# Row-tiled low query products, h read in PSUM, weights' words through ScalarE and a PSUM bank, and a new order list

## The chip, the cores and the metric

One program runs on one core of a Trainium2 chip. The metric is the device time of one execution in microseconds (us). The core's engines work side by side, each through its own queue in order: TensorE (PE), VectorE (DVE), ScalarE (ACT), GpSimd (POOL) and SyncE (SP, which here issues DMAs). SBUF is the big on-chip memory, PSUM the small one that TensorE writes, in banks of 512 f32 words per partition.

## The reference, cut to what matters

```
q_pool = q.reshape(B, H, S//2, 2, D).mean(axis=3)            # B=4, H=8, S=1152, D=64
scores = (q_pool @ k^T) / 8                                    # 576 x 1152 for each head
attn   = softmax(scores) ;  x = attn @ v                       # 2304 tokens x 512
h = x @ w_in                                                   # 512 -> 2048
P = a0 + a1 h + a2 h^2 + a3 h^3 ;  Q = 1 + |b0||h| + |b1| h^2
y = (P / (Q + 1e-6)) @ w_out                                   # 2048 -> 512
e = argmax(y @ w_gate) ;  gate = softmax(...)[e] ; eom = sigmoid(y @ w_output_gate)[e]
out = gate * eom * (relu(y @ w1[e]) @ w2[e])                   # top-1 of 8 experts, 512 -> 1024 -> 512
```

The arithmetic is that of f32: each f32 operand is cut into a high and a low f16 part, and a product is the sum of high·high, high·low and low·high.

## The kernel before, in words

**Attention** runs in 144 units. A unit is one head's 128 queries against all 1152 keys, and two neighbouring units (t = 0 and 1) are the two heads of a pair; 128 units are of this kind, and 16 ("m" units) hold the last 64 queries of two heads, each with its own 64 columns of TensorE. A unit's 1024 first scores go to one of two score buffers of two banks each (`sab`, in turn; line 718), the last 128 to a third bank (`shared`). VectorE finds their maximum (lines 728 and 731), ScalarE or VectorE makes the bias (738, 740), ScalarE takes exp (746). The exponentials are cut into high (`ph`, 755/757) and low (`pl`, 761), transposed by a DMA that SP issues (763), and multiplied by v (770). K and q are likewise cut (520 high, 526 low) and transposed by DMA (529). K's high and low lie one above the other in the 128 contraction rows, so a unit takes q_high against both, and q_low against both: four matmuls of 512 columns, each with all 128 rows.

**The first expert layer** takes 18 tiles of 128 tokens, each in 4 groups of 512 hidden columns, 72 groups in all. A group's h comes from 48 small matmuls (1148 to 1150) in one of two banks `hps`. It is copied to SBUF (1189, on ScalarE or VectorE). The numerator's steps `lin`, `tt` and `next_` (1172/1174, 1163, 1184 to 1187) work on that copy, on VectorE, GpSimd or (lin) ScalarE, while ScalarE takes Abs, Square, Ln and Exp in the PSUM bank itself (1197 to 1203). Three more VectorE steps (1159) follow, then the cut into gh and gl (1207, 1163) and the product with w_out (1215 to 1217). The weights are stored as 64-bit floats, and three VectorE steps over 1024 words turn a chunk into f32 (881, 884, 888; 16 chunks, 48 instructions); high and low parts follow.

**The second expert layer** works on 128 tokens of one expert at a time ("slots"). Some come while the first layer runs; 14 late slots follow at the end, in plain code: 96 matmuls of 128 columns (1476 to 1478), ReLU (1483) and its rest (1484) over 1024 columns, 24 matmuls of 512 columns (1494 to 1496), the gate (1506), and an indirect DMA of the rows (1500). Beside them the next expert's weights are sized (478, an all-reduce on GpSimd at 1443, the scale at 1422 to 1424) and cut (500, 511).

**What sets the order.** Up to the late slots every engine follows one long list, `ORDER`: each entry is an engine's letter (T for TensorE, V for VectorE, A for ScalarE, G for GpSimd, S for SP) and a number of a step, and the list both chooses the engine of a step and its place. Waits between engines come from what steps read and write. TensorE does not reorder: a matmul that waits holds up those behind it.

Of the kernel before, what the change touches and what calls it, by code (L numbers as in the profile page):

```python
# [9 lines left out]
F32 = mybir.dt.float32  # L10
F16 = mybir.dt.float16
BF16 = mybir.dt.bfloat16
I32 = mybir.dt.int32
AF = mybir.ActivationFunctionType
ALU = mybir.AluOpType
# [7 lines left out]
G2 V4 S7 A96 G97 V3 S0 V1 A11 V12 V13 V14 S38 V15 V16 S37 S8 V17 V18 S30 V39 V40 V86 V41 A42 V87 G88 A90 V19 V20 V21  # L23
V22 S52 V23 V24 A89 V43 S51 V25 V26 V53 S31 S9 A120 V27 V32 V28 V54 V33 V29 S10 S44 S65 S66 V55 V121 S45 V34 A123 V124
A56 V57 S91 A35 V4018 V36 S6 V67 V46 A93 V68 V47 V48 A49 V69 A70 S58 V94 V50 S59 S79 V71 S80 S126 A155 S95 T109 V60
V61 V81 V62 A63 V156 V82 S73 V64 V83 S72 V74 V75 V76 A84 S158 A184 V185 A77 S125 A152 S92 S213 V78 T98 V100 T99 V101
S5 A102 A103 A104 A105 T110 V111 S214 G153 V215 S122 T127 V112 V113 V216 A114 G394 T128 A115 S157 V129 G106 S220 V130
A181 V217 A131 A132 V85 T138 A116 G117 V140 A218 T139 V141 A133 S154 A142 A143 V4019 T159 T160 A144 V182 T170 A395
A397 S221 V222 V223 V287 V161 G396 A398 V219 V162 S107 A134 A163 S227 V224 S228 V229 V230 A225 S118 V135 V231 V226
A145 V146 A165 S234 S235 V236 A232 V237 S4017 g233 V4022 S183 T108 T119 A164 T171 V172 V173 V174 S241 T188 V190 A176  # L30
S242 S187 S136 A175 T189 S147 V191 A1079 V238 S255 S248 V192 g166 V243 V244 A239 T199 V201 T137 T148 S249 A177 V167
S168 A193 T200 V245 S263 V149 V202 V150 V151 A194 A246 V203 V240 V247 G178 V250 V251 V252 V274 S256 S399 S179 V273
A204 V275 V276 A205 A195 G196 T402 T401 V257 V258 S186 V1080 A253 T169 V254 S262 A206 g207 T180 S1082 V259 A1076 g1077
V403 V404 V405 A406 T412 V414 V278 T413 V277 A260 A407 V279 V280 T423 S197 T198 A408 V264 V265 S208 V409 V266 A267
# [12 lines left out]
V687 V688 V697 T352 A689 V681 T353 T696 G370 T545 S671 A690 V546 S682 V547 g691 T371 T372 G692 V548 A1072 V698 T709
A549 V699 A700 V550 T373 T374 T672 T710 A701 A702 G703 A375 G391 T720 V711 V712 V713 T376 A715 S551 V722 A377 V286
T683 T378 A714 T721 V716 V379 V723 S693 V724 S704 T731 A725 G717 A726 T552 V380 V381 V382 T383 V733 V727 T694 T553
A384 T732 V385 A386 T573 T742 V734 V735 A736 G728 V387 A737 T743 V389 G738 G739 V390 V744 T705 V706 T869 V745 A746  # L50
A747 A748 T554 T555 V707 V871 V708 S718 T719 A556 T870 A557 V1304 A559 T880 A558 V872 V873 T574 G749 g750 A874 A562
S1074 A1305 A875 A563 V392 V882 T881 V883 V884 V560 T575 S729 T576 V577 A578 T891 V388 G1306 A886 g393 g876 S740 G877
T730 S1107 T902 S751 V561 A885 T892 V564 V565 A580 T741 S878 V566 V893 V894 A567 S1310 A1307 T594 T595 A579 T596 T597
A887 A1308 V895 A896 T903 A897 V1137 G1138 A583 A598 A898 T752 V888 S889 T916 V904 V905 A906 V581 g899 V568 V753 A599
T569 A907 A584 g601 V754 V755 T879 V918 A908 V582 S1142 S900 S1139 A756 T917 g757 S758 V919 V585 A909 T927 V586 A920
g910 A921 A922 g923 T928 V587 A600 T890 V929 V930 T570 V931 A604 T938 A605 T615 V602 T571 V606 T616 T572 A588 A932
g589 S911 T939 A933 V603 A1108 T901 V940 A934 g935 V924 V607 V941 A942 A943 V608 T949 V951 A609 G1464 V1109 A944 S925
A1166 T590 T617 T950 T591 S1309 T592 G610 V952 V953 T618 V619 A945 A620 g622 T759 T912 A954 A955 A956 V1167 T1083 S936
# [285 lines left out]
def whole(tc, general, keep, checked, q, k, v, w_in, w_out, moe_a, moe_b, w_gate, w_ogate, w1, w2, out):  # L344
# [1309 lines left out]
    if not general:  # L1654
        make_fixed(-7)
# [213 lines left out]
```

## Time and profile before

| | us |
|---|---|
| runs | 1105.92, 1108.17, 1108.96 (median 1108.17) |
| profiled execution: time | 1104.09 |
| profiled execution: span of the trace | 1102.2 |
| TensorE busy | 923.3 (84%) |
| VectorE busy | 868.2 (79%) |
| ScalarE busy | 726.6 (66%) |
| GpSimd busy | 566.3 (51%) |

The mean granted clock of TensorE is 0.951. The shares are means over stages: a start of 55 us, attention with the first layer up to about 860 us, and the late slots. TensorE's matmuls overlap, and a matmul's printed duration (0.38 us for 512 columns) is longer than the distance from one start to the next (0.22 us).

### The profile page before, as it was taken

The page shows a single profiled execution, that of the slowest core. Times are in us where ns is not written, and L with a number is a line of the kernel's source. Part 1 is how long each engine was busy: PE and PEld are TensorE (multiplying, and loading weights), DVE is VectorE, ACT ScalarE, POOL GpSimd, SP SyncE. Part 2 cuts the span into 40 slices and gives each one's busy share as a digit, 9 for nine tenths or more (in the row PEclk, how much of TensorE's full clock was granted, in tenths as well). Part 3 has the DMA queues.
Part 4 walks back from the last instruction along what each step waited for, and adds up shares of the span by engine and source line. Part 5 has one row for each costly group of instructions (what it writes and reads, how often), then busy time and mean ns, then how long its engine had stood idle before and what let it go on. Part 6 is the DMA issues. An engine that isn't in the chain of part 4 may idle for free. (4 is left out here: it accounts for less than half of the span.)

```text
span 1102.2 us, 30178 instructions
## 1 busy us (share of the span) xinstructions
PE 923.3 (84%) x12138; PEld 660.7 (60%) x12138; DVE 868.2 (79%) x1727; ACT 726.6 (66%) x1132; POOL 566.3 (51%) x396
## 2 busy tenths in 40 slices
PE   0144678877789999999998889999999998999984
PEld 0022555655557766777776657677777675776742
DVE  6998888888888999998998998998898843333452
ACT  2364578777779888898887888899877511222222
POOL 1034267785568766667776567686845611010110
PEclk9955699999899999999999999999999999999997
DMA  8899999999999999899999999999864324333530
GB/s 300 269 252 286 222 194 190 195 212 210 203 191 172 208 186 203 170 158 179 158 193 178 188 171 187 218 152 163 145 111 147 76 59 98 78 73 74 174 87 17
DMA packets 493493, 185.91 MB, mean 169 GB/s; under 512 B 454596, under 2 KB 473028, under 8 KB 493253
## 3 DMA queue, kind: packets, MB, share of 16 engines
q1 hardware_dynamic: 490365, 174.26, 81.5%
q0 software_dynamic: 2960, 9.46, 2.5%
q8 instruction: 99, 1.62, 0.6%
q14 instruction: 69, 0.57, 0.2%
HBM read 60.45 MB, written 11.82 MB: 66 GB/s over the span
## 5 line engine op out<-in xcount | busy, mean ns | idle before, releaser
L1148 PE MATMUL hps<-scr,winh 128*128 128x128 f16 x1152 | 210.1, 222 | 9.1 <-DVE scr L1159 7.0
L1149 PE MATMUL hps<-scr,winh 128*128 128x128 f16 x1152 | 210.0, 222 | 0.0
L1150 PE MATMUL hps<-scr,winl 128*128 128x128 f16 x1152 | 209.9, 222 | 0.0
L761 POOL TENSOR_TENSOR att<-att 128x1152 f16<-128x1152 f32 x69 | 169.3, 2453 | 52.3 <-ACT att L755 27.6
L718 PE MATMUL sab<-att 128*128 128x512 f16 x512 | 138.9, 397 | 54.0 <-DMA att<-att 46.5
L728 DVE TENSOR_REDUCE small<-sab 128x1 f32<-128x1024 f32 x144 | 175.1, 1217 | 10.9 <-PE sab L718 8.1
L770 PE MATMUL shared<-att 128*128 128x65 f16 (+3 forms) x4320 | 151.0, 198 | 38.9 <-DMA att<-att 21.5
L770 PEld LDWEIGHTS <-att 128*128 128x128 f16 (+1 forms) x4320 | 141.0, 103 | 65.0 <-DMA att<-att 32.0
L746 ACT ACTIVATE att<-sab,small 128x1024 f32<-128x1024 f32 x144 | 159.9, 1111 | 12.8 <-DVE small L740 9.5
L718 PEld LDWEIGHTS <-att 128*128 128x128 f16 x768 | 69.8, 101 | 143.8 <-issue 62.2
L1149 PEld LDWEIGHTS <-winh 128*128 128x128 f16 x1152 | 113.8, 99 | 27.7 <-issue 11.6
L1163 POOL TENSOR_TENSOR scr<-scr 128x512 f16<-128x512 f32 (+1 forms) x77 | 103.4, 1345 | 48.3 <-ACT scr L1207 18.2
L1148 PEld LDWEIGHTS <-winh 128*128 128x128 f16 x1152 | 114.5, 99 | 19.5 <-issue 2.2
L1150 PEld LDWEIGHTS <-winl 128*128 128x128 f16 x1152 | 113.8, 99 | 0.0
L1476 PE MATMUL sab<-att 128*128 128x128 f16 x608 | 106.0, 221 | 7.0 <-DMA att<-att 4.9
L1215 PE MATMUL yps<-wouth,scr 128*128 128x512 f16 x288 | 109.9, 381 | 2.0 <-DVE small L493 1.4
L1217 PE MATMUL yps<-wouth,scr 128*128 128x512 f16 x288 | 109.8, 381 | 1.7 <-POOL scr L1163 1.3
L1216 PE MATMUL yps<-woutl,scr 128*128 128x512 f16 x288 | 109.8, 381 | 0.0
L1478 PE MATMUL sab<-att 128*128 128x128 f16 x608 | 105.9, 221 | 2.4 <-DVEq L1732 1.8
L1477 PE MATMUL sab<-att 128*128 128x128 f16 x608 | 105.9, 221 | 0.0
L1500 POOL DMA_INDIRECT out_dram<-att x19 | 19.0, 997 | 164.3 <-ACTq L1732 116.3
L755 ACT CAST att<-att 128x1152 f16<-128x1152 f32 x66 | 76.1, 1153 | 20.3 <-DMA att<-att 19.5
(219 smaller groups left out, 2250.9 us busy)
## 6 DMA issues: line engine op xcount, KB each, us to landing
att<-in_k_dram SPq DMA_DIRECT2D x16, 576.0 KB, 5.0
att<-in_q_dram SPq DMA_DIRECT2D x16, 512.0 KB, 4.7
att<-in_moe_w_dram SPq DMA_DIRECT2D x4, 2048.0 KB, 8.9
att<-in_v_dram SPq DMA_DIRECT2D x14, 576.0 KB, 4.8
scr<-in_moe_w_out_dram SPq DMA_DIRECT2D x12, 512.0 KB, 4.7
att<-ysort SPq DMA_DIRECT2D x19, 257.0 KB, 2.7
scr<-in_moe_w_in_dram SPq DMA_DIRECT2D x8, 512.0 KB, 8.5
woutl<-in_moe_w_in_dram SPq DMA_DIRECT2D x6, 512.0 KB, 7.5
```

The lines of the kernel that those rows point to most:

```text
L718: T.matmul(dst[:, d0:d0 + w], qT[:, H * x + 2 * i + t, :], rhs, start=(x == 0), stop=(x == 1))
L728: A(key - ahead - .6, {"DVE": 1.13}, lambda e: V.tensor_reduce(out=mm[:, 0, bi:bi + 1], in_=ab, axis=AX.X, op=MAX, negate=True), r=[f"sab{ ...
L746: return lambda e: S.activation(dst, src, AF.Exp, bias=mm[:, 2, bi:bi + 1], scale=escale)
L761: lambda e: eng(e).tensor_tensor(out=phs[pb][:, 1], in0=p32, in1=ph(), op=SUB),
L770: T.matmul(pvb[p0:p0 + w, bi, 0:d], pt[:, lhs, p0:p0 + w], rhs[:, h, c, :], start=(c == 0 and lhs == 0 and rhs is vh), stop=(lhs == 2 * KC ...
L1148: T.matmul(hp, wh, xh[:, kc, :], start=(kc == 0), stop=False)
L1149: T.matmul(hp, wh, xl[:, kc, :], start=False, stop=False)
L1150: T.matmul(hp, wl, xh[:, kc, :], start=False, stop=(kc == KD - 1))
L1215: T.matmul(yps, a, wouth[:, ff, :], start=(ff == 0), stop=False)
L1216: T.matmul(yps, a, woutl[:, ff, :], start=False, stop=False)
L1217: T.matmul(yps, b_, wouth[:, ff, :], start=False, stop=(ff == KF - 1))
L1476: T.matmul(o, a, xT[:, kc], start=(kc == 0), stop=False)
```

## The change

It is one diff with several parts:

- Weights' words: a chunk is worked in two halves of 512. ScalarE makes the exponent's offset from the top 16 bits, one VectorE step writes into the PSUM bank `yps`, a second reads it back and writes f32 to SBUF. So a chunk takes two ScalarE and four VectorE instructions of 512 words for three VectorE instructions of 1024.
- Groups: the copy of h is gone; `lin`, `tt` and `next_` read the PSUM bank, `tt` and `next_` on VectorE alone, `lin` on ScalarE or VectorE. Abs goes from the bank to SBUF, Square and Ln stay there, Exp comes back to the bank. A token `hx` keeps readers of the same bank one after the other.
- Scores: K's parts are laid out so that head 0 has its high part in rows 0 to 63 and head 1 in rows 64 to 127. `high` is q_high against all 128 rows, as before. `low` is q_low against K's high part alone, 64 rows: head 0 from rows 0 to 63 into `sab0`, head 1 from rows 64 to 127 into `sab1`, matmul by matmul in turn. The low products of both heads stand with the second head's high ones in one step. The product low·low is dropped. For the first 128 queries of a batch q_low is not doubled.
- Late slots: the first product comes in two halves in alternate banks, with ReLU and rest for each half of 512; the scale of the next weights is made with their cut (`[2 * p:...]`) and not with their size, so a slot's VectorE steps no longer stand behind the all-reduce; the last slot's rows are written by an indirect DMA at the very end of the program, in both branches of its last If.
- Constants are set in two steps, and the index tables lie in another buffer.
- `ORDER` is a new list.

```diff
-V22 S52 V23 V24 A89 V43 S51 V25 V26 V53 S31 S9 A120 V27 V32 V28 V54 V33 V29 S10 S44 S65 S66 V55 V121 S45 V34 A123 V124
+A3386 V3113 V2907 A3107 T2921 T2922 V3108 A2908 A2909 S3083 T3062 V2910 A2923 A2924 V3063 V3114 G3092 T2753 T2754
...
+            kn4 = nrm.rearrange("p (c x d) -> p c x d", c=KC, x=4)
...
+            A(key + .4, {"DVE": 0.73, "ACT": 1.15, "POOL": 1.25}, as16(kn4[:, :, 0:4:3, :], krc), r=tk, w=tn)
+            A(key + .5, {"DVE": 1.33, "POOL": 2.5}, rest(kn4[:, :, 1:3, :], krc, kn4[:, :, 0:4:3, :]), r=tk + tn, w=tl)
...
+        def high(dst, h, ps, stop=False):
...
+                    T.matmul(dst[:, d0:d0 + w], qT[:, 2 * i + h, :], krow(h, c0, w), start=True, stop=False)
...
+        def low(dsts, ps):
+            for c0, w in ps:
+                d0 = c0 % 1024
+                for h, dst in dsts:
...
+                        T.matmul(dst[:, d0:d0 + w], qT[64 * h:64 * h + 64, lo, :], krow(h, c0, w, 64 * h, 64),
+                                 start=False, stop=True)
...
-        A(key - ahead - 1.2, {"PE": 0.86 * f2}, smm(ab, [(0, 512), (512, 512)]), r=ins, w=[f"sab{par}"])
...
+        elif t == 0:
+            A(key - ahead - 1.2, {"PE": 0.43}, lambda e: high(sab[0], 0, main), r=ins, w=["sab0"])
+            A(key - ahead - 1.1, {"PE": 1.06},
+              lambda e: (high(sab[1], 1, main), low([(0, sab[0]), (1, sab[1])], main)), r=ins, w=["sab1", "sab0"])
...
+                return [lambda e: S.activation(hx.bitcast(U16)[:, 0:1024:2], top, AF.Copy, scale=2.0**-13, bias=2.0**-14 - 0.5),
+                        lambda e: V.scalar_tensor_tensor(out=ax, in0=high[:, cs], scalar=3, in1=hx,
+                                                         op0=ALU.logical_shift_left, op1=ALU.bitwise_xor),
+                        lambda e: V.scalar_tensor_tensor(out=di[:, cs], in0=high[:, cs], scalar=-0x80000000, in1=ax,
+                                                         op0=ALU.bitwise_and, op1=ALU.bitwise_xor)]
...
-        A(k2, {"ACT": 0.48, "DVE": 0.6}, lambda e: (S.copy if e == "ACT" else V.tensor_copy)(tq, hb),
-          r=[ht], w=[f"tq{tb}"], port=0)
...
-        A(k2 + .04, LP, lin, r=[f"tq{tb}", c], w=[f"tp{tb}"])
-        A(k2 + .045, {"POOL": 1.24, "DVE": 0.6}, tt(tp, tp, tq, MUL), r=[f"tq{tb}"], w=[f"tp{tb}"])
-        A(k2 + .05, {"POOL": 1.9, "DVE": 0.65}, next_, r=[f"tq{tb}", c], w=[f"tp{tb}"])
+            A(k2 + .01, {"ACT": 0.57}, lambda e: S.activation(te, hb, AF.Abs, scale=cf("sh")), r=[ht, c], w=[tk] + hx)
...
+            A(k2 + .03, {"ACT": 0.62, "DVE": 0.6}, lin, r=[ht, c], w=[pk] + hx, port=0)
+            A(k2 + .04, {"DVE": 0.6}, tt(tp, tp, hb, MUL), r=[ht], w=[pk] + hx)
+            A(k2 + .05, {"DVE": 0.65}, stt(tp, tp, lambda: cf("n1"), hb, ADD, MUL), r=[ht, c], w=[pk] + hx)
...
+            A(k2 + .07, {"ACT": 0.5}, lambda e: S.activation(hb, lg, AF.Exp, scale=-1.0), r=["lg"] + hx, w=[ht])
...
+            steps = mms_[0:4] + relu(halves[0], 0, 512) + mms_[4:8] + relu(halves[1], 512, 512)
...
-                do(wsplit(s, x)[3 * p:None if p else 3])
+                do(wsplit(s, x)[2 * p:None if p else 2])
...
+    with short.Else():
+        do([({"POOL": 1.05}, put_last)])
```

On VectorE, near the program's start, the first chunks of weights' words stand like this before (lines 881, 884 and 888 are the three steps, 526 a low part):

```order
L881 TENSOR_SCALAR scr<-woutl 128x1024
L884 SCALAR_TENSOR_TENSOR scr<-woutl,scr 128x1024
L632 TENSOR_TENSOR att<-att 128x8x64
L888 SCALAR_TENSOR_TENSOR scr<-woutl,scr 128x1024
L522 CAST att<-att 128x8x64
L493 RECIPROCAL small<-small 128x1
L493 TENSOR_SCALAR small<-small 128x1 x4
L493 TENSOR_REDUCE small<-small 128x1
L526 TENSOR_TENSOR winl<-scr,winh 128x1024
```

And now, at the same place of VectorE's order:

```order
L943 SCALAR_TENSOR_TENSOR yps<-wouth,att 128x512
L478 TENSOR_REDUCE small<-small 128x1
L945 SCALAR_TENSOR_TENSOR scr<-wouth,yps 128x512
L943 SCALAR_TENSOR_TENSOR yps<-woutl,att 128x512
L945 SCALAR_TENSOR_TENSOR scr<-woutl,yps 128x512
L943 SCALAR_TENSOR_TENSOR yps<-woutl,att 128x512
L945 SCALAR_TENSOR_TENSOR scr<-woutl,yps 128x512
L478 TENSOR_REDUCE small<-winh 128x1
L511 SCALAR_TENSOR_TENSOR winl<-scr,winh 128x1024
```

The second step of a half reads the bank that the first has just written, and the next half writes it again, so these steps follow one another in one chain. Before the first `TENSOR_REDUCE` of scores stand 33 such half steps, 7 low parts of w_in and 3 of K or v; before the change there were 24 whole steps, 7 low parts of w_in and 5 of K or v.

On TensorE, in the middle of the attention, the scores of a unit stand between second products of the first layer before (`sab0_74` and `sab1_75` are the two score buffers):

```order
L1217 MATMUL yps_79<-wouth_72,scr_83 128x512
L718 LDWEIGHTS att_81
L718 MATMUL sab0_74<-att_81 128x512
L718 LDWEIGHTS att_81
L718 MATMUL sab0_74<-att_81 128x512
L718 LDWEIGHTS att_81
L718 MATMUL sab0_74<-att_81 128x512
L718 LDWEIGHTS att_81
L718 MATMUL sab0_74<-att_81 128x512
L1215 LDWEIGHTS scr_83
```

And now the second step of a pair of units, whose two other high products into `sab0_74` stand further up:

```order
L741 LDWEIGHTS att_81
L741 MATMUL sab1_75<-att_81 128x512
L741 LDWEIGHTS att_81
L741 MATMUL sab1_75<-att_81 128x512
L752 LDWEIGHTS att_81
L752 MATMUL sab0_74<-att_81 128x512
L752 LDWEIGHTS att_81
L752 MATMUL sab1_75<-att_81 128x512
L752 LDWEIGHTS att_81
L752 MATMUL sab0_74<-att_81 128x512
L752 LDWEIGHTS att_81
L752 MATMUL sab1_75<-att_81 128x512
```

Four full matmuls for one unit have become six for the second half of a pair, the last four of them on 64 rows and into the two buffers in turn; `sab0` is complete only when this step is.

On VectorE, in a late slot, this stood before (478 sizes the next weights, 1422 to 1424 make their scale, 1484 is the rest of ReLU):

```order
L478 TENSOR_REDUCE small<-winh 128x1
L1422 TENSOR_SCALAR small<-small 128x1
L1423 TENSOR_SCALAR small<-small 128x1
L1424 TENSOR_SCALAR small<-small 128x1
L1732 UNCONDITIONAL_BRANCH x2
L1484 SCALAR_TENSOR_TENSOR att<-sab_75,att 128x1024
L1485 TENSOR_SCALAR small<-att,small 128x1
```

And now:

```order
L478 TENSOR_REDUCE small<-att 128x1
L1827 UNCONDITIONAL_BRANCH x2
L1563 SCALAR_TENSOR_TENSOR att<-sab_74,att 128x512
L1563 SCALAR_TENSOR_TENSOR att<-sab_75,att 128x512
L1572 TENSOR_SCALAR small<-att,small 128x1
L1826 TENSOR_LOAD att
L1826 ISA x2
L1827 COMPARE_AND_BRANCH
L1500 TENSOR_SCALAR small<-small 128x1
```

The scale's three steps have moved from ahead of the slot's rest to behind it, and the rest comes in two halves.

Over the part that the list orders, the steps that moved most are (instructions before and after): on VectorE `pl` 47 and 23, `ph` 15 and 9, low parts of K and v of 1152 columns 22 and 13, `tt` 44 and 72, `next_` 58 and 72, `lin` 18 and 28, copies of h 16 and 0, evacuations of `yps` (1322, 1328) 16 and 8; on ScalarE copies of h 56 and 0, `ph` 102 and 72, `lin` 30 and 44, words 0 and 32; on GpSimd `pl` 97 and 121, `ph` 27 and 63, parts of K and v of 1152 columns 10 and 25, and 80 steps of groups (`lin`, `tt` and the two of `next_`) to none.

## Rows read from the trace of the kernel before

**Rows 1.** Windows: stretch, length, busy PE, PEld, DVE, ACT, POOL, clock, DMA share, GB/s:

```profile
0.00:55.00 55.00, 3.79 (x10) 1.52 (x11) 45.00 (x74) 18.41 (x20) 4.28 (x11) 0.97 0.86 284
55.00:300.00 245.00, 170.28 (x2305) 118.56 (x2304) 207.66 (x368) 170.39 (x258) 138.72 (x81) 0.84 1.10 218
300.00:860.00 560.00, 533.26 (x7490) 387.25 (x7491) 515.43 (x1059) 478.05 (x781) 387.52 (x273) 0.99 0.96 174
860.00:1080.00 220.00, 207.77 (x2313) 150.56 (x2310) 95.92 (x223) 58.13 (x75) 34.82 (x32) 0.99 0.37 86
1080.00:1103.00 23.00, 8.17 (x24) 2.80 (x24) 4.20 (x7) 1.63 (x3) 0.97 (x1) 0.70 0.05 13
```

**Rows 2.** Groups of TensorE, 55 to 300: busy, mean ns, idle before, what ended it:

```profile
L770 PE MATMUL shared<-att 128*128 128x65 f16 (+3 forms) x1269 | 49.0, 204 | 30.2 <-DMA att<-att 18.2 <-DVE small L731 5.3 <-DMA att<-scr 4.6
...
L718 PE MATMUL shared<-att 128*128 128x128 f16 x78 | 11.6, 235 | 20.5 <-ACT att L746 18.2 <-DMA att<-scr 1.8 <-DVE small L493 0.4
```

**Rows 3.** Line 728: ns min/median/max, first and last start:

```profile
L728 DVE TENSOR_REDUCE small<-sab x144: 1193/1217/1225, 55.5 to 808.2; 128x1 f32<-128x1024 f32 x144
```

**Rows 4.** Time line of VectorE (start us, duration us, what), first weights' words:

```profile
14.59 0.69 DVE L881 TENSOR_SCALAR scr<-woutl 128x1024 int32<-128x1024 int32 x1
15.32 1.22 DVE L884 SCALAR_TENSOR_TENSOR scr<-woutl,scr 128x1024 int32<-128x1024 int32 x1
```

**Rows 5.** Time line of TensorE, first matmuls ([idle before <-what ended it]):

```profile
44.13 3.57 PE L718 MATMUL sab<-att 128*128 128x512 f16 x8 [44.13 <-DMA att<-att]
```

**Rows 6.** Time line of TensorE, one unit's scores:

```profile
424.16 1.03 PE L718 MATMUL sab<-att 128*128 128x512 f16 x4
```

**Rows 7.** Time line of TensorE, the scores of an m unit:

```profile
488.99 0.38 PE L1217 MATMUL yps<-wouth,scr 128*128 128x512 f16 x1
489.29 1.05 PE L715 MATMUL sab<-att 128*64 128x512 f16 x8
490.28 0.39 PE L1215 MATMUL yps<-wouth,scr 128*128 128x512 f16 x1
```

**Rows 8.** Groups of VectorE by shape, 0 to 860:

```profile
L1187 DVE SCALAR_TENSOR_TENSOR scr<-scr,small 128x512 f32<-128x512 f32 x56 | 55.2, 986 | 0.2
...
L1159 DVE SCALAR_TENSOR_TENSOR scr<-scr,hps 128x512 f32<-128x512 f32 x70 | 47.9, 684 | 1.6
L761 DVE TENSOR_TENSOR att<-att 128x1152 f16<-128x1152 f32 x31 | 46.7, 1506 | 1.9 <-ACT att L755 1.9
...
L1174 DVE TENSOR_SCALAR scr<-scr,small 128x512 f32<-128x512 f32 x18 | 12.7, 703 | 2.5 <-ACT scr L1189 1.3 <-POOL scr L761 1.1
...
L1322 DVE TENSOR_SCALAR yr<-yps 128x512 f32<-128x512 f32 x9 | 6.2, 686 | 2.0 <-PE yps L1217 1.9
```

**Rows 9.** Groups of ScalarE by shape, 0 to 860:

```profile
L746 ACT ACTIVATE att<-sab,small 128x1024 f32<-128x1024 f32 x144 | 159.9, 1111 | 12.8 <-DVE small L740 9.5 <-DVE small L493 1.2 <-DVE att L761 1.1
L755 ACT CAST att<-att 128x1152 f16<-128x1152 f32 x66 | 76.1, 1153 | 20.3 <-DMA att<-att 19.5 <-ACT att L746 0.2
...
L1189 ACT COPY scr<-hps 128x512 f32<-128x512 f32 x55 | 32.2, 586 | 22.0 <-PE hps L1150 21.7
```

**Rows 10.** Groups of GpSimd by shape, 0 to 860:

```profile
L761 POOL TENSOR_TENSOR att<-att 128x1152 f16<-128x1152 f32 x69 | 169.3, 2453 | 52.3 <-ACT att L755 27.6 <-DVE att L757 8.6 <-DVE scr L1163 2.5
...
L1163 POOL TENSOR_TENSOR scr<-scr 128x512 f32<-128x512 f32 x28 | 39.3, 1405 | 8.8 <-DVE scr L1174 4.4 <-DVE small L493 2.2 <-DVE hps L1159 1.5
```

**Rows 11.** Time line of TensorE, the late slots:

```profile
1053.75 0.22 PE L1476 MATMUL sab<-att 128*128 128x128 f16 x1 [3.18 <-DMA att<-att]
...
1081.82 0.39 PE L1494 MATMUL hps<-att 128*128 128x512 f16 x1 [2.25 <-ACTq L1732]
...
1083.86 0.61 PE L1496 MATMUL hps<-att 128*128 128x512 f16 x1 [1.31 <-DVE att L1484]
...
1090.92 0.38 PE L1496 MATMUL hps<-att 128*128 128x512 f16 x1
```

**Rows 12.** Time line of VectorE, a scale in a late slot:

```profile
1052.56 0.15 DVE L1422 TENSOR_SCALAR small<-small 128x1 int32<-128x1 int32 x1 [4.53 <-POOL small L1443]
```

More of the change, by code (lines that the diff above doesn't have):

```diff
@@ L13 @@
 I32 = mybir.dt.int32
+U16 = mybir.dt.uint16
 AF = mybir.ActivationFunctionType
@@ L616, in prep_row @@
         buf = nrmQ[0] if own else nrm
-        qh, ql = (buf[:, x * n:(x + 1) * n].rearrange("p (h o d) -> p h o d", o=2, d=D) for x in range(2))
-        qT = qTs[r % 2][:, 0:2 * nh, :]
+        single = not general and r == 0
+        ol = 1 if single else 2
+        nq = n * (2 + ol) // 2
+        qh, ql = (buf[:, a:z].rearrange("p (h o d) -> p h o d", o=y, d=D) for a, z, y in ((0, n, 2), (n, nq, ol)))
+        qT = qTs[r % 2][:, 0:nq // 128, :]
         f = nh / 8.0
@@ L724, in unit @@
         f2 = 1.15 if is_m else 1
[L725 to L726 removed]
+        main, end = [(0, 512), (512, 512)], [(1024, 128)]
+        if general:
+            A(key - ahead - 1.2, {"PE": 0.86 * f2}, smm(ab, main), r=ins, w=[f"sab{par}"])
+        elif is_m:
+            A(key - ahead - 1.2, {"PE": 0.99}, smm(ab, main), r=ins, w=[f"sab{par}"])
+        elif t == 0:
+            A(key - ahead - 1.2, {"PE": 0.43}, lambda e: high(sab[0], 0, main), r=ins, w=["sab0"])
+            A(key - ahead - 1.1, {"PE": 1.06},
+              lambda e: (high(sab[1], 1, main), low([(0, sab[0]), (1, sab[1])], main)), r=ins, w=["sab1", "sab0"])
+        if not general and r == 0:
+            A(key - ahead - .5, {"PE": 0.31}, lambda e: (high(sc_, t, end), low([(t, sc_)], end)), r=ins, w=["X"], bank=1)
+        else:
+            A(key - ahead - .5, {"PE": 0.23 if is_m else 0.11}, smm(sc_, end), r=ins, w=["X"], bank=1)
         mt = [] if bi == 0 else [f"mm{bk % 4}"]
@@ L821, in whole @@
     scr = keep("one", [128, KD * DFF], F32, name="scr")
+    odd = [mix[:, 512 * x:512 * x + 512] for x in range(2)]
     stage = [scr[:, 2048 * x:2048 * x + 2048].bitcast(I32) for x in range(3)]
@@ L1093, in whole @@
     tps = [cut(W, F32, f"tp{x}") for x in range(NTB)]
-    tw = cut(W, F32, "tw")
-    tqs = [cut(W, F32, f"tq{x}") for x in range(NTB)]
+    tw = cut(W, F32, "tw", "te0")
+    tqs = [cut(W, F32, f"tq{x}", ["te1", "lg"][x]) for x in range(NTB)]
     ghs, gls = ([cut(W // 2, F16, f"{nm}{x}") for x in range(NGB)] for nm in ("gh", "gl"))
@@ new lines, in group @@
+            A(k2 + .045, {"POOL": 1.24, "DVE": 0.6}, tt(tp, tp, tq, MUL), r=[f"tq{tb}"], w=[f"tp{tb}"])
+            A(k2 + .05, {"POOL": 1.9, "DVE": 0.65}, next_, r=[f"tq{tb}", c], w=[f"tp{tb}"])
+            A(k2 + .06, {"ACT": 0.61}, lambda e: S.activation(hb, tw, AF.Ln, bias=cone), r=["tw"], w=[ht])
+            A(k2 + .07, {"ACT": 0.5}, lambda e: S.activation(hb, hb, AF.Exp, scale=-1.0), w=[ht])
+            A(k2 + .08, {"DVE": 0.65}, stt(tw, tw, lambda: cone, hb, ADD, MUL), r=[ht], w=["tw"])
@@ L1469, in slot_g1 @@
         hp = sab[s % 2]
+        halves = hbs if s % 2 else [a[:, 0:512] for a in sab]
         def mm(fc):
             def f(e):
-                o = hp[:, fc * 128:(fc + 1) * 128]
+                o = hp[:, fc * 128:(fc + 1) * 128] if s < NEARLY else halves[fc // 4][:, fc % 4 * 128:(fc % 4 + 1) * 128]
                 for kc in range(KD):
```

561 lines of the change are left out of this document (304 added, 257 removed).

## The prediction

> **What bounds the kernel now.** I read the windows first [rows 1], because the page's shares are means over unlike stages. In the first 55 us VectorE is busy for 45.00, TensorE for 3.79. From 55 to 300 VectorE is busy for 207.66 of 245 us (85%), TensorE for 170.28, so TensorE stands still for 74.7. From 300 to 860 it is the other way round: TensorE 533.26 of 560, idle 26.7; VectorE is close behind with 515.43. In the late slots only TensorE counts (207.77 of 220), and in the last 23 us a tail runs at a granted clock of 0.70.
>
> Then I read what ends TensorE's idle time between 55 and 300 [rows 2]: 30.2 us before the product with v, 18.2 of them until a transposing DMA has landed, and 20.5 before the last 128 scores, 18.2 until ScalarE's exp is through. So the chain of a unit (maximum, exp, cut, transpose) sets the pace there; VectorE, ScalarE and GpSimd each hold a piece of it. The unit's maximum runs 144 times from 55.5 to 808.2 [rows 3], which is 10.45 us for each of 72 pairs.
>
> **The start, -6 us.** TensorE's first score begins at 44.13, when K's transpose has landed [rows 5], but the first maximum runs only at 55.5, since VectorE has weights' words in its queue ahead of it. A chunk's words cost 0.69 + 1.22 and a third step of 1.22 (as the second), 3.13 us [rows 4]; 24 such steps, 8 chunks, make 25.0. Now 33 half steps stand there. None is in the trace: an integer step that writes PSUM. Nearest are a 512-wide step with one PSUM operand, 0.684 [rows 8], and the dependent pair of rows 4, which starts 0.73 apart at a duration of 0.69. 33 x 0.73 = 24.1; two low parts of K or v fewer (1152 wide, 1.506 in rows 8) give -3.0. With -0.9 from the words that is -3.9; the constants that wait for GpSimd's index tables no longer stand ahead, worth some 2 more by my estimate. Bounds: +3 (a half step takes 0.82 instead of 0.73) and -10 (the first maximum right behind the first scores). ScalarE has 18.41 busy us of 55 [rows 1], so the new steps there (32 of about 0.59, the time of its 512-wide copy in rows 9) are covered.
>
> **55 to 300, -10 us.** From the counts of the list, VectorE loses 24 `pl` and 9 low parts of K and v (33 x 1.506 = 49.7), 16 copies of h and 8 evacuations (24 x 0.686 = 16.5), and gains 28 `tt`, 14 `next_` and 10 `lin`: 52 x 0.684 = 35.6. The 58 `next_` that it had, at a mean of 0.986 for the very same work from SBUF [rows 8], come to about 0.72 if a PSUM operand makes them as even as line 1159 is: -15. The 16 chunks' words: 64 x 0.73 = 46.7 for 50.1, -3. Sum about -49, and some -15 for small items (`ph`, cuts of early weights, biases), as an estimate: -64 of the 723 us between 55 and 860. Its share by time in this stretch is 245/805, so -20. VectorE is 85% busy here and holds only a part of the idle time's enders: I take half, -10. ScalarE loses 56 copies (0.586) and 30 `ph` (1.153) and gains 14 `lin` and the words, -33 in the same 805 us, by [rows 9]: it was not the last here, so I give nothing for it. Bounds 0 and -30.
>
> *A rule against it.* Line 1174, a scaled sum from SBUF, takes 0.703; line 1322, the like from PSUM, 0.686 [rows 8]. The Trainium skill, "VectorE: DVE Perf Modes", section "Why PSUM operands drop a tier", says that a PSUM operand closes the mode that uses both SBUF read ports and leaves f32 at the slowest rate; by that, `lin` from the old copy would cost half of `lin` from PSUM, and 28 of them would lose about 28 x 0.35 = 10 us here. The two rows show no such gap (line 1174 ran beside other engines' traffic), so the sum leaves it out.
>
> **300 to 860, -13 us.** Here TensorE is the bound, so only its columns and its last idle time count. Four score matmuls start 0.216 apart ((1.03 - 0.38)/3 [rows 6], 0.38 being one matmul's printed time [rows 7]); a pair of units takes 8 x 0.216 = 1.73. Now it is 4 full ones, two pairs of half-height ones, and a change of tiling and back. Row tiles are not in the trace; the nearest thing is the m unit, whose 64-column tiles run two at a time: 8 matmuls in 0.99, and 0.30 from the matmul before instead of 0.216 [rows 7]. So two tiles share 0.216, and going in and out costs (0.30 - 0.216) + (0.99 - 0.864) = 0.21. A pair then takes 6 x 0.216 + 0.21 = 1.51, 0.22 less; 64 pairs give -14.2, of which 560/805 fall here: -10. If tiles of rows run one after another, the pair takes 1.94 and the 64 pairs cost +13.4. I take the m unit's behaviour, as it is the nearest row. Of the 26.7 idle us I take 3, since VectorE and ScalarE come earlier. Bounds for the stretch: +10 and -25.
>
> *A rule that makes it smaller.* The m unit's tiles ran at twice the speed [rows 7]. The Trainium skill, "TensorE: Matmul & The Clock Gate", section "Measured speedup vs the span model", has 3.07 for four row tiles, 77% of the ideal; at 77% of two, a pair of tiles would take 0.28 instead of 0.216 and the 64 pairs would give about -6 instead of -14. By that the whole sum would be some 8 less; no run before shows it.
>
> Groups lose a copy of 0.586 ahead of their chain, and gain waits: readers of the bank now take turns, Abs, `lin`, `tt`, `next_`, then Exp. The 48 matmuls of the next group use the other bank; 72 groups over some 750 us leave 10 us each, so I cost this at nothing. If that cover is gone, TensorE would show waits for line 1159's successor.
>
> **Late slots, -4 us.** VectorE's wait of 4.53 us for the all-reduce [rows 12] had only the rest of ReLU behind it, and TensorE's own gap there, 3.18, ended with a DMA [rows 11]: nothing for that. In the last slot TensorE stands 2.25 and 1.31 us for ReLU and its rest, and then its 24 matmuls start over 9.1 us (1081.82 to 1090.92) where 23 x 0.216 is 5.0; the granted clock of the stretch is 0.70 [rows 1, 11]. With halves, the second half alone is late: I take half of 3.56, -1.8, and half of the 4.1 that the clock costs, -2. Bounds +3 (the last indirect DMA stands behind one branch more) and -12.
>
> **Sum.** -6 - 10 - 13 - 4 = -33 us. The profiled execution took 1104.09 (its span 1102.2), 4 us under the median of the runs shown; 1104.09 - 33 = 1071, from the median 1075. I say 1073.
>
> **The rivals.**
> *The row tiles give nothing, or the relief ends nowhere* (1095). The tiles cost as much as they save (0 instead of -14), or 24 `pl` that moved from VectorE (1.506) to GpSimd (2.453, [rows 8, 10]) hold the product with v back: 24 x 0.95 = 23 us. GpSimd's 526 us of 805 rise: 24 x 2.453 + 36 `ph` and 15 parts of K and v at 1.2 to 2.45 each, about +130, less 80 group steps of at most 1.405, -112 at most, so 544 to 600 (up to 75%). For it: 30.2 us of waits before line 770 already. Against it: GpSimd has 200 us free, and the list chose these engines anew. The sum would lose about 20: 1093 to 1097.
> *The score buffers become one* (slower). `sab0` is complete only after the step that also needs `sab1`. So TensorE, which keeps its order, holds that step, and the groups' matmuls behind it, until the second unit's exp of the pair before is done; then both maxima (2 x 1.22), bias and exp (1.11) and the scores (1.51) run in a row. With about 1 for the small steps, that is 2.44 + 1 + 1.11 + 1.51 = 6.1 us for a pair against a period of 10.45 [rows 3, 9]. For it: 18.2 us of TensorE's waits end with exp even with independent buffers [rows 2]. Against it: the period leaves 4.4 us. It decides from 33/72 = 0.46 us more for each pair; at 0.75 it costs 54, net +21: 1125.
> *All of the idle time goes* (1050): the idle 74.7 between 55 and 300 falls by 25 and not by 10, the 26.7 behind it by 10. For it: VectorE and ScalarE both get about 5 to 9% freer; against it: transposing DMAs end most of the waits, at a DMA share of 1.10 there [rows 1], and nothing in the change lightens them.
>
> **How the numbers follow.** Forecast (1058 to 1089, its own range) 0.56; all idle goes 0.10; tiles or relief give nothing 0.19, of which 0.04 end within 0.3% of before; buffers coupled 0.11, of which 0.01 the same; another wait of the new list that eats just the gain 0.04, half the same and half slower. A measurement of this kernel can tell 0.3%, 3.3 us, from no change. Faster 0.56 + 0.10 + 0.15 = 0.81, same 0.04 + 0.01 + 0.02 = 0.07, slower 0.10 + 0.02 = 0.12. The range for 8 in 10 runs from 1048 to 1102: it takes in most of the first rival and leaves the coupled buffers and the best corner out.
>
> **What would show it.** The first maximum near 49 and the last near 785. Low score matmuls starting in pairs that share about 0.22 us; if each takes 0.22 alone, the columns term is wrong by its sign. VectorE's busy time near 800 in all, GpSimd's near 620. `next_` near 0.74 and words near 0.7: a half step at 0.8 or more would undo the start's term. TensorE's idle time from 300 on under 25 us; if waits for exp before `sab` grow beyond some 20 us in all, the buffers are coupled. In the last slot, the gaps before the second product under 2 us and its 24 matmuls in less than 8; if the granted clock falls as before, half of the late term is gone. The forecast is wrong as a whole if TensorE's busy time falls and its idle time rises by as much.

## The result, and the profile after

The changed kernel takes 1078.38 us (median of 4 runs, 1075.60 to 1080.02) against 1108.57 for the kernel before. The ratio is 0.9722, with a 95% interval of 0.9695 to 0.9750: 31 us less, 28 to 34. The profiled execution took 1075.60, its span is 1073.8. The forecast was 1073, range 1048 to 1102.

Busy time over the whole span: TensorE 907.3 us (before 923.3), VectorE 822.3 (868.2), ScalarE 706.2 (726.6), GpSimd 601.7 (566.3). The windows after, in the stretches and columns of [rows 1]:

```profile
0.00:55.00 55.00, 3.75 (x12) 1.04 (x12) 42.80 (x89) 30.39 (x40) 6.28 (x13) 1.00 0.99 305
55.00:300.00 245.00, 182.00 (x2479) 120.36 (x2480) 211.83 (x386) 179.42 (x271) 157.74 (x88) 0.95 1.08 215
300.00:860.00 560.00, 527.92 (x7544) 376.19 (x7541) 484.25 (x1059) 442.73 (x729) 417.27 (x279) 0.99 0.95 175
860.00:1080.00 220.00, 193.61 (x2112) 137.31 (x2109) 83.38 (x202) 53.70 (x79) 20.42 (x22) 0.97 0.34 83
```

From 55 to 300, TensorE is busy for 11.7 us more and runs 174 matmuls more in the same time, at a granted clock of 0.95 instead of 0.84. From 300 to 860 it is idle for 32.1 us, where it was for 26.7. Line 772, the maximum of the first scores, shows how the rest splits; it answers to [rows 3]:

```profile
L772 DVE TENSOR_REDUCE small<-sab x144: 1199/1218/1227, 51.6 to 782.8; 128x1 f32<-128x1024 f32 x144
```

The first maximum comes 3.9 us earlier, the last 25.4, so 21.5 us lie between them; 3.0 more come behind the last, since the span is 28.4 shorter. What limits the first maximum is on VectorE's time line:

```profile
48.38 0.69 DVE L943 SCALAR_TENSOR_TENSOR yps<-wouth,att 128x512 int32<-128x512 int32 x1
49.09 0.17 DVE L878 MEMSET ones<- 128x128 bf16 x1
51.57 0.07 DVE L880 MEMSET att<- 128x18 f16 x1 [2.31 <-POOL att L526]
51.60 1.22 DVE L772 TENSOR_REDUCE small<-sab 128x1 f32<-128x1024 f32 x1
```

The last of these words in the queue ahead of the maximum was through at 49; then constants that the list puts there waited 2.31 us for GpSimd's low part of v. A pair's scores on TensorE (first its first half, then, of another pair, the second half and what follows):

```profile
409.11 0.59 PE L741 MATMUL sab<-att 128*128 128x512 f16 x2
409.54 0.22 PE L1215 MATMUL hps<-scr,winh 128*128 128x128 f16 x1
...
411.16 0.59 PE L741 MATMUL sab<-att 128*128 128x512 f16 x2
411.68 0.61 PE L752 MATMUL sab<-att 64*128 64x512 f16 x4
412.22 0.39 PE L1292 MATMUL yps<-wouth,scr 128*128 128x512 f16 x1
```

0.43 for the first two, 0.52 for the next two with the change of tiling, 0.54 for the four low ones: 1.49 us for a pair, where the prediction worked out 1.51. The groups of the engines that answer to [rows 8 to 10]:

```profile
L1226 DVE SCALAR_TENSOR_TENSOR scr<-scr,small,hps 128x512 f32<-128x512 f32 x140 | 103.7, 742 | 9.7 <-ACT hps L1280 8.0
...
L1230 DVE TENSOR_TENSOR scr<-scr,hps 128x512 f32<-128x512 f32 x70 | 47.7, 681 | 0.6
L805 DVE TENSOR_TENSOR att<-att 128x1152 f16<-128x1152 f32 x21 | 28.8, 1375 | 1.8 <-ACT att L799 1.8
L1242 DVE TENSOR_SCALAR scr<-hps,small 128x512 f32<-128x512 f32 x28 | 22.5, 805 | 8.4 <-ACT scr L1274 8.1
L943 DVE SCALAR_TENSOR_TENSOR yps<-scr,att 128x512 int32<-128x512 int32 x20 | 18.7, 935 | 1.0
```

```profile
L790 ACT ACTIVATE att<-shared,small 128x128 f32<-128x128 f32 x144 | 52.6, 365 | 46.0 <-DVE small L784 28.5 <-PE shared L814 9.7 <-issue 1.4
...
L942 ACT ACTIVATE att<-scr 128x512 uint16<-128x512 uint16 x20 | 15.5, 774 | 10.7 <-DMA scr<-in_moe_w_out_dram 6.0 <-DVE yps L943 4.0 <-ACT winh L500 0.7
```

`next_` (among line 1226's first group, all of whose steps take 0.72 to 0.75) went from a mean of 0.986 to 0.742 and `tt` takes 0.681, as forecast. The mean of 0.986 hides two kinds of steps. Before (ns min/median/max, then one of the long steps and what GpSimd did beside it):

```profile
L1187 DVE SCALAR_TENSOR_TENSOR scr<-scr,small x58: 732/746/3546, 139.8 to 866.9; 128x512 f32<-128x512 f32 x58
405.02 2.79 DVE L1187 SCALAR_TENSOR_TENSOR scr<-scr,small 128x512 f32<-128x512 f32 x1
...
404.88 2.37 POOL L761 TENSOR_TENSOR att<-att 128x1152 f16<-128x1152 f32 x1
```

So the usual step was as fast before, and what went were the long ones: 10 of 58 took 0.9 to 3.5 us, and each of the ten overlaps a GpSimd instruction; the one shown ends 0.55 us behind it. That VectorE waited for GpSimd there is my reading; no run separates it. Writing the words to PSUM (`scr` to `yps`) has a mean of 0.935, above the 0.73 taken, but a median of 0.701; the words' step on ScalarE takes 0.774, where the prediction took 0.59.

### The profile page after: what moved, and what is told of

Same layout as the page of the kernel before. It is cut to its first block, busy times and chain, and to the rows that moved or that the text cites. A ratio compares the mean times of both kernels' runs of the same rounds, so it can differ in the third digit from the quotient of the medians.

```text
span 1073.8 us, 30231 instructions
## 1 busy us (share of the span) xinstructions
PE 907.3 (84%) x12138; PEld 634.9 (59%) x12138; DVE 822.3 (77%) x1735; ACT 706.2 (66%) x1117; POOL 601.7 (56%) x401
## 5 line engine op out<-in xcount | busy, mean ns | idle before, releaser
L805 POOL TENSOR_TENSOR att<-att 128x1152 f16<-128x1152 f32 x79 | 192.7, 2439 | 60.5 <-ACT att L799 23.1
L1215 PE MATMUL hps<-scr,winh 128*128 128x128 f16 x1152 | 208.1, 221 | 7.4 <-DMA scr<-scr 4.1
L1216 PE MATMUL hps<-scr,winh 128*128 128x128 f16 x1152 | 207.7, 220 | 0.0
L1217 PE MATMUL hps<-scr,winl 128*128 128x128 f16 x1152 | 207.7, 220 | 0.0
L741 PE MATMUL sab<-att 128*128 128x512 f16 x256 | 80.8, 403 | 54.9 <-DMA att<-att 47.9
L1226 DVE SCALAR_TENSOR_TENSOR scr<-scr,small,hps 128x512 f32<-128x512 f32 x144 | 106.6, 742 | 9.7 <-ACT hps L1280 8.0
L805 POOL TENSOR_TENSOR scr<-att,scr 128x1152 f16<-128x1152 f32 x42 | 101.7, 2422 | 20.4 <-ACT scr L799 7.7
L1230 POOL TENSOR_TENSOR scr<-scr 128x512 f16<-128x512 f32 x53 | 64.3, 1213 | 33.3 <-ACT scr L1284 17.9
L790 ACT ACTIVATE att<-shared,small 128x128 f32<-128x128 f32 x144 | 52.6, 365 | 46.0 <-DVE small L784 28.5
L775 DVE TENSOR_SCALAR_CACHE_REDUCE small<-shared,small 128x128 bf16<-128x128 f32 x144 | 50.1, 348 | 25.8 <-PE shared L814 10.6
L1555 PE MATMUL sab<-att 128*128 128x128 f16 x384 | 66.3, 219 | 2.6 <-DMA att<-att 1.9
```

The lines of the kernel that those rows point to most:

```text
L741: T.matmul(dst[:, d0:d0 + w], qT[:, 2 * i + h, :], krow(h, c0, w), start=True, stop=False)
L790: return lambda e: S.activation(dst, src, AF.Exp, bias=mm[:, 2, bi:bi + 1], scale=escale)
L805: lambda e: eng(e).tensor_tensor(out=phs[pb][:, 1], in0=p32, in1=ph(), op=SUB),
L1215: T.matmul(hp, wh, xh[:, kc, :], start=(kc == 0), stop=False)
L1216: T.matmul(hp, wh, xl[:, kc, :], start=False, stop=False)
L1217: T.matmul(hp, wl, xh[:, kc, :], start=False, stop=(kc == KD - 1))
```

## The experiments

Ratios are to the kernel before on the same chip. Differences are to the changed kernel's 0.9722 and carry both intervals (that is the uncertainty given with them); 0.001 is 1.1 us.

**Row tiles: three runs.** `low_full`:

```diff
-                        T.matmul(dst[:, d0:d0 + w], qT[64 * h:64 * h + 64, lo, :], krow(h, c0, w, 64 * h, 64),
+                        p0, np_ = (64 * h, 64) if r == 0 else (0, 128)
+                        T.matmul(dst[:, d0:d0 + w], qT[p0:p0 + np_, lo, :], krow(h, c0, w, p0, np_),
```

> The changed kernel with the low products of 48 of the 64 pairs at full height again (128 rows, low times low included, no row tiles); order and everything else as changed. Theory (row tiles run side by side and TensorE's columns end the time): a pair takes 1.73 us instead of 1.49, 48 pairs give +11, the time goes from 0.972 of before to 0.982. Rival (the columns are hidden, the gain is VectorE's relief): at most +3, 0.975.

Measured: 0.9764 (0.9729 to 0.9799), +4.7 us with an uncertainty of 5. The four low matmuls take 0.86 us, with no change of tiling ahead of them:

```profile
412.73 0.59 PE L741 MATMUL sab<-att 128*128 128x512 f16 x2
413.16 1.03 PE L753 MATMUL sab<-att 128*128 128x512 f16 x4
414.02 0.38 PE L1293 MATMUL yps<-wouth,scr 128*128 128x512 f16 x1
```

In the trace 60 of the 64 pairs run at full height, not 48: the edit's condition keeps row tiles for the first four pairs of the program alone. (They are also the only ones whose q_low is not doubled, not the first 128 queries of every batch.) So 60 pairs cost TensorE 0.23 us each, 13.8 us, and the time shows 0.34 of it, with anything from none to 0.7 within the uncertainty. `low_serial`:

```diff
-            for c0, w in ps:
-                d0 = c0 % 1024
-                for h, dst in dsts:
+            for h, dst in dsts:
+                for c0, w in ps:
+                    d0 = c0 % 1024
```

> The changed kernel with the same row-tiled matmuls, but head 0's two first and head 1's two after them instead of in turn. Theory (two tiles share 0.216 us only when they stand next to each other): the four low matmuls of a pair come apart in time, up to 4 x 0.216 instead of 2 x 0.216, +0.43 for each of 64 pairs, +27 us at most, 0.997 of before; with one of the four borders still shared +0.22, +14. Rival (TensorE overlaps them anyhow, or the columns are hidden): no change, 0.972.

Measured: 0.9744 (0.9714 to 0.9774), +2.4 us with an uncertainty of 4.5, no change that can be told; +14 and +27 are out. The four matmuls take 0.54 us again:

```profile
411.00 0.61 PE L752 MATMUL sab<-att 64*128 64x512 f16 x4
411.54 0.39 PE L1292 MATMUL yps<-wouth,scr 128*128 128x512 f16 x1
```

My theory that they must stand in turn is wrong. In the trace the four start at 0.00, 0.01, 0.23 and 0.23 us, so still in pairs; in the changed kernel it is 0.00, 0.00, 0.23 and 0.23. `low_same_rows` tells why:

```diff
-qT[64 * h:64 * h + 64, lo, :], krow(h, c0, w, 64 * h, 64),
+qT[0:64, lo, :], krow(h, c0, w, 0, 64),
```

> The changed kernel with both heads' low products on rows 0 to 63 (head 1 then takes K's low part, so its scores are not the reference's). It tells why four low matmuls take 0.54 us in either order. If two row halves work side by side, all four on one half take 4 x 0.216 + 0.1 = 0.96 us. If a matmul of 64 rows is simply twice as fast, they take 0.54 again.

Measured: 1089.71 us, one run without an interval, and 0.97 us for the four:

```profile
414.25 1.03 PE L752 MATMUL sab<-att 64*128 64x512 f16 x4
415.22 0.39 PE L1292 MATMUL yps<-wouth,scr 128*128 128x512 f16 x1
```

That is 4 x 0.216 + 0.1, and the four start at 0.00, 0.23, 0.44 and 0.66, one by one. So the halves of the array work side by side, a matmul of 64 rows by itself is no faster, and the way back to full tiles costs 0.1. TensorE's 27 us more of columns (64 x 0.42) cost some 15 us of time by its ratio to the same chip's kernel before, 0.54 of them, from a single run.

**What each engine's time is worth: three runs.** An instruction that gives the same result when it is repeated is issued twice in each group. All three stand in a group's chain, so a worth found here need not hold for a step elsewhere.

```diff
-            A(k2 + .10, {"DVE": 0.64}, stt(tp, te, -2.0, hb, ADD, MUL), r=[tk, ht], w=[pk])
+            A(k2 + .10, {"DVE": 0.64}, lambda e: [stt(tp, te, -2.0, hb, ADD, MUL)(e) for _ in range(2)], r=[tk, ht], w=[pk])
```

> The changed kernel with the last of the three steps on line 1226 issued twice in each of 72 groups (same result): about 53 us more on VectorE, all else the same. It is the reverse of VectorE's relief (46 us between the two profiles). Theory (VectorE holds a part of the chain, a third to a half of its time is seen): +16 to +27 us, 0.987 to 0.997 of before. Rival (TensorE ends all): under +5.

Measured: 0.9919 (0.9893 to 0.9946), +22 us (uncertainty 4) for 55.3 us more of VectorE's busy time: 0.39. The maxima tell where it falls; this run's, against 782.8 for the last one of the changed kernel:

```profile
L772 DVE TENSOR_REDUCE small<-sab x144: 1199/1218/1227, 51.4 to 806.8; 128x1 f32<-128x1024 f32 x144
```

The last maximum comes 24.0 us later, the 49th only 3.1 (308.4 and 305.2), so some 21 us of it fall behind 300 us.

```diff
-            A(k2 + .01, {"ACT": 0.57}, lambda e: S.activation(te, hb, AF.Abs, scale=cf("sh")), r=[ht, c], w=[tk] + hx)
+            A(k2 + .01, {"ACT": 0.57}, lambda e: [S.activation(te, hb, AF.Abs, scale=cf("sh")) for _ in range(2)], r=[ht, c], w=[tk] + hx)
```

> The changed kernel with Abs issued twice in each of 72 groups (same result): about 49 us more on ScalarE, all else the same. The prediction gave nothing for ScalarE's relief. By that: under +5 us (0.972 to 0.977 of before). Rival (ScalarE's exp is in the chain of the units, so its time counts like VectorE's): +15 to +25 us.

Measured: 0.9849 (0.9797 to 0.9901), +14 us (uncertainty 6.5) for 44.4 us more: 0.32. The rival holds; the prediction's zero for ScalarE does not.

```diff
-        A(k2 + .12, {"POOL": 1.13, "DVE": 0.6}, tt(gl, tp, gh, SUB), r=[f"tp{tb}", f"gh{gb}"], w=[f"gl{gb}"])
+        A(k2 + .12, {"POOL": 1.13, "DVE": 0.6}, lambda e: [tt(gl, tp, gh, SUB)(e) for _ in range(2 if e == "POOL" else 1)], r=[f"tp{tb}", f"gh{gb}"], w=[f"gl{gb}"])
```

> The changed kernel with the low part of g issued twice where GpSimd makes it (53 groups, same result): about 64 us more on GpSimd. The prediction held that GpSimd's load, up by 35 us between the two profiles, costs nothing. By that: under +5 us. Rival (GpSimd, now busy for 575 of 805 us, is near its bound, since each low part of the exponentials waits behind it): +15 us or more.

Measured: 0.9799 (0.9751 to 0.9847), +8.5 us (uncertainty 6) for 65.3 us more: 0.13, between the two theories; at 2.4 to 14.6 us it does not settle the first.

**The late slots: three runs on the kernel before.** `late_only` has the late slots' part of the diff alone, `put_only` of that the end of the program alone, `slots_only` the other half:

```diff
+    with short.Else():
+        do([({"POOL": 1.05}, put_last)])
```
```diff
+            steps = mms_[0:4] + relu(halves[0], 0, 512) + mms_[4:8] + relu(halves[1], 512, 512)
-                do(wsplit(s, x)[3 * p:None if p else 3])
+                do(wsplit(s, x)[2 * p:None if p else 2])
```

> The kernel before with the changed late slots alone (halves, scale made with the cut, last rows written at the end); the list and all that it orders as before. The prediction's step says -4 us, 0.996 of before. Rival, read from the trace of the changed kernel (in the last slot the cut of the weights now waits for the scale, so ReLU is as late as before; idle time of the late slots 15 us in both): no change within 1 us.

> The kernel before with the last slot's rows written at the very end of the program, and nothing else changed. Theory (between the gate of the last slot and the end of the span 10.7 us pass before and 6.9 us where the late slots are changed; the last indirect DMA no longer stands ahead of the last branch): -4 us, 0.9965 of before. Rival (the halves and the scale give what the late slots gave): no change.

> The kernel before with the late slots' halves, banks and the scale made with the cut, but the last rows written where they were. Theory (idle time of TensorE in the late slots stays about 15 us): -1 us, 0.999 of before. Rival (the prediction's step): -4 us, 0.996.

Measured: `late_only` 0.9948 (0.9925 to 0.9971), -5.7 us; `put_only` 0.9960 (0.9939 to 0.9981), -4.4; `slots_only` 1.0007 (0.9980 to 1.0033), no change that can be told, and -4 is out. My rival for `late_only` was wrong: I had read only TensorE's idle time, and the gain lies behind TensorE's last matmul. Time line of ScalarE, the gate of the last slot, with the span on the line ahead: before, `slots_only`, `put_only` and the changed kernel.

```profile
core 0 of [0], span 1102.2 us
...
1091.46 0.69 ACT L1506 ACTIVATE att<-hps,small 128x512 f32<-128x512 f32 x1 [10.52 <-PEq L1802]
```
```profile
core 0 of [0], span 1099.8 us
...
1089.01 0.69 ACT L1521 ACTIVATE att<-yps,small 128x512 f32<-128x512 f32 x1 [8.50 <-PE yps L1510]
```
```profile
core 0 of [0], span 1099.7 us
...
1093.60 0.69 ACT L1521 ACTIVATE att<-hps,small 128x512 f32<-128x512 f32 x1 [10.90 <-PEq L1818]
```
```profile
core 0 of [0], span 1073.8 us
...
1067.16 0.69 ACT L1598 ACTIVATE att<-yps,small 128x512 f32<-128x512 f32 x1 [9.00 <-PEq L1897]
```

From the gate to the end it is 10.7 and 10.8 us where the rows go out ahead of the last branch, 6.1 and 6.6 where they go out behind it. GpSimd issues the rows some 1 us behind the gate in all four; from that issue to GpSimd's last drain pass 5.9 us before and 1.2 in `put_only`, and from the drain to the end 3.9 in both.

**The start and the last slot: three runs on the changed kernel.** `early_consts` moves one entry of the list:

```diff
-S46 S8 V5 g3 V34 S0 V2 A12 A124 V13 V14 V15 V16 S36 V17 V18 V19 V20 V21 V22 S35 A37 V23 V24 V25 V26 V27 V28 S3997
+S46 S8 V5 V1 g3 V34 S0 V2 A12 A124 V13 V14 V15 V16 S36 V17 V18 V19 V20 V21 V22 S35 A37 V23 V24 V25 V26 V27 V28 S3997
-A113 S123 T126 g125 T127 S153 V1 V129 S252 S251 A180 S186 T128 V130 A131 A132 T138 V245 A133 A212 S261 g213 V247 V4
+A113 S123 T126 g125 T127 S153 V129 S252 S251 A180 S186 T128 V130 A131 A132 T138 V245 A133 A212 S261 g213 V247 V4
```

> The changed kernel with one entry of the list moved: the constants that VectorE writes just ahead of the first maximum stand at the list's start. In the changed kernel they wait 2.3 us there for GpSimd's low part of v (first maximum at 51.6 instead of 49.2). Theory (the start counts one to one): first maximum at 49.3, -2.3 us, 0.970 of before. Rival (the first units have slack behind them): first maximum early, time unchanged.

Measured: first maximum at 48.9, ratio 0.9709 (0.9661 to 0.9757), -1.4 us with an uncertainty of 6: it can't tell -2.3 from nothing. `last_scale`:

```diff
-                do(wsplit(s, x)[2 * p:None if p else 2])
+                cut = 3 if s >= NFULL else 2
+                do(wsplit(s, x)[cut * p:None if p else cut])
```

> The changed kernel, but for the slots from the 18th on the scale of the weights is made with their size again and not with their cut. Theory (in the last slot ScalarE's four cuts wait 1.9 us for the scale and hold ReLU up): TensorE's gap before the last second product falls from 3.0 to about 1.2 us, the gap behind it from 0.9 to under 0.9, -2 to -3 us, or -5 if the clock then stays up. Rival (the gap is set by the loading of the weights): no change.

Measured: 0.9733 (0.9675 to 0.9791), +1 us with an uncertainty of 7, which settles nothing by itself. The gap ahead of the last second product fell from 3.00 only to 2.57, and the one behind it from 0.93 to 0.13. Both edits in one:

> The changed kernel with the constants at the list's start and, in the slots from the 18th on, the scale made with the size: the two edits of the runs before in one, as a candidate for the fastest. If they add: -2 to -4 us against the changed kernel, 0.969 to 0.970 of before. Rival (the slack behind the start and the state of the clock at the end swallow both): 0.972.

Measured: 0.9738 (0.9716 to 0.9760), +1.8 us with an uncertainty of 4: -4 is out, -2 at the edge. The rival is the likelier; no version tried here beats the changed kernel beyond its interval.

## Why the prediction was right, and where its terms were not

**The sum.** -33 was forecast, -30.2 measured between the medians. With what the doubled instructions showed, the busy times of the two profiles make it up: VectorE -45.9 x 0.39 = -18; ScalarE -20.4 x 0.32 = -6.5; GpSimd +35.4 x 0.13 = +4.6; TensorE's columns 64 x -0.23 x 0.34 (`low_full`, 4.7 of 13.8) = -5; the rows at the end -4.4. That is -29, with an uncertainty of some 8 from those of its terms. The worths were measured by adding work to the changed kernel, and that they hold in reverse and add up is assumed, so the agreement to a microsecond is luck; only that VectorE's term is the largest is clear of the uncertainties. The forecast's own closeness is in part luck too: a columns term that was too big made up for relief of VectorE and ScalarE that it left out. No run takes h in PSUM, the weights' words or the new list alone, so what each of these gave stays open.

**The start, -6.** The first maximum moved by 3.9. The half steps cost what was taken there (0.69, some 0.75 apart), the two low parts went, and a new wait of 2.31 us for GpSimd came in, which the prediction did not look for. Nor did the lead last. The 49th maximum, before and after, starts at the same time:

```profile
305.22 1.23 DVE L728 TENSOR_REDUCE small<-sab 128x1 f32<-128x1024 f32 x1 [1.40 <-PE sab L718]
305.25 1.22 DVE L772 TENSOR_REDUCE small<-sab 128x1 f32<-128x1024 f32 x1
```

So the units have not kept a microsecond of it by 300 us, and the whole 25.4 us by which the last maximum is earlier arise behind that.

**55 to 300, -10.** Here TensorE gained 11.7 us of work. The units did not become faster: 48 maxima had run by 300 us in both kernels. What filled the time were groups of the first layer:

```profile
L1215 PE MATMUL hps<-scr,winh 128*128 128x128 f16 x229 | 40.3, 220 | 2.5 <-DVE scr L1226 2.1 <-DMA scr<-scr 0.4
```

229 of these matmuls, where the same window before held 192: a group has 16 of each of its three lines, so the groups are 2.3 ahead. The clock is not what did it: from 55 to 110 us it was 0.51 before and 1.00 after, but in the profile of `low_serial` it was 0.55, and there the 49th maximum starts at 304.1 and the groups are as far. The factor of a half for VectorE's relief was measured as 0.39 over the whole.

**300 to 860, -13.** The mechanism was right: 1.49 us for a pair instead of 1.73, where 1.51 was worked out, two row tiles in the time of one. The Trainium skill, "TensorE: Matmul & The Clock Gate", section "Measured speedup vs the span model", has 3.07 for four row tiles; by that share of the ideal a pair would take 0.28, as an estimate. Half of 0.54 less the 0.1 of the way back is 0.22, so this trace shows the full factor of two. The size was wrong: "Here TensorE is the bound, so only its columns and its last idle time count". `low_full` took 13.8 us of columns back and cost 4.7, so the 10 of the stretch were nearer 3 (5 by `low_same_rows`). The rest of the 25 us that the last maximum gained here is most likely relief of other engines: some 21 of the 22 us that `dve_twice` cost fall in this stretch, where the prediction gave 3 for VectorE and ScalarE together. TensorE's idle time, forecast to fall under 25 us, is 32.1. A stretch in which an engine is busy for 95% need not be bound by that engine alone.

**ScalarE, 0.** This step failed: "it was not the last here, so I give nothing for it". Its time is worth about as much as VectorE's (0.32 and 0.39), which makes 6.5 us, with an uncertainty of 3.

**GpSimd.** Its load rose to 575 us of 805 between 55 and 860, within the 544 to 600 of the rival; the 24 x 0.95 us of that rival did not come. By 0.13 its 35 us more cost 4.6, with an uncertainty of some 3.

**h in PSUM.** By the Trainium skill, "VectorE: DVE Perf Modes", section "Why PSUM operands drop a tier", `lin` should double, as an estimate. The prediction set this aside because two means, 0.703 and 0.686, showed no gap [rows 8]. The mean of 0.703 was the wrong number to read. Before and after, in ns min/median/max:

```profile
L1174 DVE TENSOR_SCALAR scr<-scr,small x18: 516/542/2585, 138.5 to 798.9; 128x512 f32<-128x512 f32 x18
L1242 DVE TENSOR_SCALAR scr<-hps,small x28: 781/804/811, 146.4 to 821.2; 128x512 f32<-128x512 f32 x28
```

Three of the 18 steps from SBUF took 0.72 to 2.59 us and lift the mean; the usual one takes 0.542, and 0.804 from PSUM. That is half as much again, so the direction is the page's and the size less than double: 28 x 0.26 = 7 us of VectorE's time, where the sum had nothing and the rule 10. By the means, with the long steps, it is 0.1 for each, 3 us.

**Late slots, -4.** The size was right and the cause wrong. "With halves, the second half alone is late" is the step that failed: the halves gave nothing that could be told. In the last slot both halves of ReLU stand on ScalarE behind four cuts of weights:

```profile
1052.93 4.27 ACT L500 ACTIVATE att<-att,small 128x1024 f16<-128x1024 f32 x4 [1.88 <-DVE small L1502]
1057.11 1.06 ACT L1562 ACTIVATE att<-sab 128x512 f16<-128x512 f32 x2
```

These cuts now wait 1.88 us for the scale that moved to them, so TensorE stands 3.00 and 0.93 us where it stood 2.25 and 1.31 [rows 11], and its matmuls start 0.43 us apart as before: its 24 matmuls start over 8.9 us, against 9.1 before and a forecast of under 8. Without the wait (`last_scale`) the first gap is still 2.57, so the four cuts themselves hold the halves up. The 4.4 us came from the end of the program, where the prediction had put a bound of +3.

**The rivals.** Coupled score buffers did not come: TensorE's wait for exp before `sab` is 7.4 us in all after and 10.4 before, against the 20 set as a mark. Two other marks were missed in size: VectorE's busy time, 822 us where 800 was forecast, and GpSimd's, 602 for 620. TensorE's busy time fell by 16.0 us and its idle time by 12.4, so the sign that the forecast is wrong as a whole did not come.

## What to carry to other kernels

Where several engines are busy for 75 to 95%, none of them need be the bound alone: estimate the worth of each by issuing one harmless instruction twice, look at where in the program the added time falls, and keep the uncertainty. Read a step's median beside its mean: a few long steps hid that `lin` is slower from PSUM. Read the time behind the last matmul as carefully as the idle time ahead of it: an output that goes out ahead of a last branch can hold up the end for longer than a late slot's gap. A relief on a queue helps only what stands first in it, as the halves of ReLU behind the four cuts suggest.

## What the runs showed of the hardware

Matmuls on different row halves overlap even when two of one half are issued ahead of two of the other: 0.54 us for four in either order, starting in pairs, and 0.97 when all four are on one half, starting one by one. The four runs of the changed kernel went from 1075.60 us at a mean granted clock of 0.980 to 1080.02 at 0.947, but the five of `both` do not go by the clock (1074.11 at 0.949, 1078.22 at 0.962), so how much of the spread between runs is the clock's stays open. In the last slot, after idle gaps of 3.00 and 0.93 us, matmuls start 0.43 us apart, twice the 0.216, until 1064.4, and at 0.216 again after that:

```profile
1063.95 0.63 PE L1585 MATMUL yps<-att 128*128 128x512 f16 x1
1064.37 0.47 PE L1586 MATMUL yps<-att 128*128 128x512 f16 x1
1064.68 0.38 PE L1587 MATMUL yps<-att 128*128 128x512 f16 x1
1064.90 0.38 PE L1585 MATMUL yps<-att 128*128 128x512 f16 x1
```
